# A recurrent attention block beside an MLP: both left query passes in the third segment of each four, and new orders of units and attention steps

## The chip, the cores and the metric

The kernel runs on one core of a Trainium2 chip. The metric is the time of one execution on the device in microseconds (us), read from the device. A core has a matrix engine (TensorE; PE in the profile, its weight loads PEld), two engines that work element by element (VectorE, here DVE, and ScalarE, here ACT), GpSimd (POOL), and SyncE (SP), which in this kernel only issues DMAs. PE writes its results to eight PSUM banks of 128 partitions x 512 float32 numbers. Sixteen DMA engines move data between the device's memory and the on-chip memory.

## The reference, cut to what matters

`x` has 2048 rows of 1024 numbers. Its layer norm `xn` goes into two branches, and the output is `x` plus both. Branch B is an MLP (1024 to 3584 to 1024, with a GELU). Branch A is a recurrence of 64 segments of 32 rows; each takes 8 memory rows from the one before. All tensors are bfloat16.

```python
for s in range(64):
    h = concatenate([mem, xn[32*s:32*s+32]])          # 8 + 32 rows of 1024
    q, k, v = h @ Wq, h @ Wk, h @ Wv                  # 32 heads of 128
    p = softmax(where(mask, q @ k.T / sqrt(128), -1e9))
    o = (p @ v) @ Wo                                  # back to 1024
    mem, out[s] = o[:8], o[8:]
return x + branch_A + gelu(xn @ w1 + b1) @ w2 + b2
```

Each of the four weight matrices of branch A has 1024 x 4096 numbers, 8 MB. Together they don't fit on the chip beside the rest, so a part of them is read again in every segment.

## The kernel before, in words

**Stages.** The first 402 us compute the layer norm and the MLP and store MLP plus `x` as rows to be added later. Then the 64 segments run one after the other, about 21.5 us each. The change lies in the segments (the loop over `s`, line 806 on).

**Units and passes.** The weights are cut into 64 units of 128 x 2048 numbers (512 KB). A segment uses them in seven passes: K half 0, Q half 0, K half 1, Q half 1, V half 0, V half 1, each of 8 units (`half_pass`, called as `K0`, `Q0`, `K1`, `Q1`, `V0`, `V1` in this text), and the output pass `O` with 16 units. A half is 16 of the 32 heads. One unit in a half pass is four matmuls of 32 rows, run beside each other in the four column groups of the PE array (`product`, line 830).

**Streamed and resident units.** 47 of the units stay on the chip for good. 17 are streamed in each segment: 15 by DMA, issued by SP into a ring of six slots, and two that are kept in four PSUM banks and copied by DVE into a slot (`copy_bits`, line 273, two copies of 128x512 for a unit). A slot is filled again as soon as PE has used its unit (`unit_done`, `start_stream`). The table `PLACED` says for each kind of segment at which places of each pass the streamed units stand (eight strings of eight places: the six half passes and the two halves of `O`; "S" is a streamed unit). Within a pass, units may stand in any order, since they are summed.

**Main rows and left rows.** A segment's 40 rows are not all multiplied in the segment itself. The 8 memory rows and the first 24 rows of `xn` make the 32 columns of `hT` (tile `hr_home`): the main rows. The last 8 rows of `xn` of four segments, which don't depend on the recurrence, are put together into one tile of 32 columns, `hL` (tile `hrL`): the left rows of a group. Each group of four segments therefore has, besides the four main passes of each kind, one left pass for K0, Q0, K1, Q1, V0 and V1, made for the group ahead (queries, keys) or at its beginning. A left pass has no weight traffic of its own: each unit is used a second time by four more matmuls while it is in its slot.

**The four kinds of segment.** `i4` is the segment's number modulo 4, and I call it the kind. The left passes are spread over the kinds:

| kind | left passes before | also |
|---|---|---|
| 0 | K1, V0 | |
| 1 | Q0 | the left outputs: `O` for 64 rows, not 32 |
| 2 | Q1 | |
| 3 | K0, V1 | |

Left queries of a group are held in `qL[0]` and `qL[1]`, four slots of 8 rows each. When the left pass of the next group overwrites them, slots not used yet must be saved: `keep_q` copies them into spare columns of the PSUM tile `mixed` (view `qS`), and `q_left` takes a segment's slot from `qL` or from `qS`.

**The boundary of two segments.** The last sum of `O` gives the 8 memory rows. They are added up (DVE, line 1224), turned into columns by two matmuls with an identity (`put_mem`, line 320), copied by DVE (line 330) into `hT`, and only then can the next segment's K0 begin. To fill that time, `lead_products` runs up to six resident units of a left pass of the next segment ahead: four before `put_mem` and two after it. Before the change this is done at all four boundaries of a group, with Q0, Q1, K0 and K1 left. In the last group there is nothing to lead with at the boundaries behind kinds 0, 1 and 2.

**The attention steps.** Between units PE does the small matmuls of the attention: `scores` (lines 947, 953), `sums` (985, 991) and `values` (1039, 1045), for each half. Between them ACT and DVE compute exponentials, minimum with a mask (line 977), normalised probabilities (lines 996, 999, 1012, 1017, 1024), the turned queries (`turn_q`: ACT copies at line 909, a transpose by DVE at line 914), and the copies of the values (line 1058). The left keys and queries are turned by `turn` (lines 882, 896). All engines work through their own instructions in the order in which the kernel is written down; there is no scheduler. After which unit a step stands is set by constants, one number for each kind: `SCORES_0` (in K1), `SUMS_0` (in Q1), `ATTEND` and `VALUES_0` (in V1; `attend` is `scores` of half 1 and the copy of V half 0), `SUMS_1` (in V1) and `VALUES_1` (in `O`).

**PSUM.** Three banks go round as accumulators (`new_acc`, `let_go`), one is `mixed`, four hold the kept units.

Of the kernel before, what the change touches and what calls it, by code (L numbers as in the profile page):

```python
# [11 lines left out]
U32 = mybir.dt.uint32  # L12
# [6 lines left out]
S = 2048  # L19
# [19 lines left out]
NL = SEG - NX  # L39
GRP = 4  # L40
# [14 lines left out]
MEM_AT = 20  # L55
EARLY_SEGS = 7
LEAD_FIRST = 4
SCORES_0 = (6, 6, 6, 5)
SUMS_0 = (4, 4, 4, 4)
ATTEND = (0, 0, 0, 1)  # L60
VALUES_0 = ((4, 4), (4, 4), (4, 4), (3, 5))
SUMS_1 = (6, 7, 6, 5)
VALUES_1 = (5, 5, 5, 5)
LATER = 4
# [9 lines left out]
def pass_order():  # L74
# [12 lines left out]

ORDER = pass_order()
PLACED = (
    "..SS...." ".S..S..." "S....S.." "....S..S" "....S..." "S..S...S" "...S..S." "S....S.S",  # L90
    "...SS..." ".S..S..." "..S..S.." "....SS.." ".S......" "S..S...S" "...S..S." "S....S.S",
    ".SS....." "S...S..." "S....S.." "....S..S" "....S..." "S..S...S" "...S..S." "S....S.S",
    "..SS...." ".S..S..." "S.....S." "....S..S" "....S..." "...SS..S" "...S..S." "S....S.S",
)
IS_STREAMED = {unit: PLACED[0][n] == "S" for n, unit in enumerate(ORDER)}
assert all(placed.count("S") == STREAMED for placed in PLACED)
# [24 lines left out]
def kernel(  # L121
# [52 lines left out]
    qL = [  # L174
        nc.alloc_sbuf_tensor_at(f"qL{u}", [P, 16, SEG], BF16, offset=SCRATCH + 1024 * (u + 1))[:, :, :] for u in range(2)
    ]
# [10 lines left out]
    def slab(place):  # L187
        if place in low:
            return low[place]
        return slabs.tile([P, 2048], BF16, name="u", tag=place)  # L190
# [8 lines left out]
    for j in range(4):  # L199
        q = slice(32 * j, 32 * j + 32)  # L200
# [148 lines left out]
    with tc.tile_pool(name="ma", bufs=2) as ma:  # L349
# [39 lines left out]
        for i in range(14):  # L389
            t = slab(f"w2_{i}")[:, :].rearrange("p (c d) -> p c d", d=DM)  # L390
# [14 lines left out]
        def next_of(ring):  # L405
            ring.rotate(-1)
            return ring[-1]
# [177 lines left out]
        for tg in range(4):  # L585
            last = tg == 3
            if last:
# [3 lines left out]
                h = 4 * IN_BANKS[1] + 2 * IN_BANKS[2]  # L591
# [12 lines left out]
            for fb in range(FC):  # L604
# [9 lines left out]
                u = next_of(us)  # L614
# [67 lines left out]
            else:  # L682
# [32 lines left out]
                for step in range(FC + AHEAD):  # L715
                    for t in range(4):
# [3 lines left out]
                        for nb in range(2):  # L720
                            n = 2 * t + nb
# [14 lines left out]
    with tc.tile_pool(name="late", bufs=1) as late:  # L736
# [18 lines left out]
        mixed = banks.tile([P, 512], F32, name="mixed", tag=f"bank{seg_banks[3]}")  # L755
# [4 lines left out]
        qS = there[:, 0:32 * NL].rearrange("p (i h t) -> p i h t", i=2, h=16)  # L760
# [42 lines left out]
        for s in range(NSEG):  # L803
            g, i4 = divmod(s, GRP)
            first, final = s == 0, s + 1 == NSEG
# [7 lines left out]
            more = g + 1 < NGRP  # L813
            units = ORDERS[i4]
            O_UNITS = units[48:]
            left_k = [first or (i4 == 3 and more), i4 == 0]
            left_q = [first or (i4 == 1 and more), first or (i4 == 2 and more)]
            left_v = [i4 == 0, first or (i4 == 3 and more)]
            left_o = i4 == 1 or final
            og, slot = divmod(s + 2, GRP)  # L820
# [97 lines left out]

            def q_left(u):

                if i4 >= 2 + u and more:
                    q = qS[:, i4 - 2 - u, :, :]
                else:
                    q = qL[u][:, :, NL * i4:NL * i4 + NL]
                nc.vector.tensor_copy(out=q_home[:, :, 0:NL], in_=q)
# [4 lines left out]

            def keep_q(u):

                n = 2 - u
                copy_bits(
                    mixed[:, 340:340 + 64 * n].bitcast(U32).rearrange("p (i h t) -> p h i t", i=n, h=16),
                    qL[u].bitcast(U32)[:, :, (GRP - n) * NL // 2:].rearrange("p h (i t) -> p h i t", i=n),
                )

            def scores(u):
# [191 lines left out]
            if left_q[0] and not first:  # L1131
                turn_qL(psQL, 0)
            psK1, psK1L = half_pass("K", 1, left_k[1], {SCORES_0[i4]: [lambda: scores(0)]})
            exps(0)
# [4 lines left out]
            }  # L1139
            at[4 if first else SUMS_0[i4]] = [lambda: sums(0)] + ([] if first else [lambda: q_left(1)])  # L1140
            if left_q[1] and not first:
# [25 lines left out]

            at = {0 if first else ATTEND[i4]: [attend]}
            n0, n1 = (3, 5) if first else VALUES_0[i4]
            if n0 == n1:  # L1170
# [29 lines left out]
            for n, unit in enumerate(O_UNITS):  # L1200
                t = unit_tile(unit)
# [13 lines left out]
            if not final:  # L1215
                o_sb = outM
                no = 16 if left_o else 8
                o = psX[:, 0:32 * no].rearrange("p (h e) -> p h e", e=32)
                if left_o:
                    nc.scalar.copy(out=o_sb[:, 0:no, :], in_=o)  # L1220
                else:
                    o = psX[:, 0:256].rearrange("p (h e) -> p h e", e=16)
                    flat = o_sb.rearrange("p h e -> p (h e)")[:, 0:256].rearrange("p (h e) -> p h e", e=16)
                    nc.vector.tensor_tensor(out=flat, in0=o, in1=st["folded"], op=ALU.add)
                ahead = []
                if (i4 == 3 or more) and not final:
                    hL = nxt["hL"]
                    w, u = (("Q", 0), ("Q", 1), ("K", 0), ("K", 1))[i4]
                    ahead = [i for i in range(KT) if not IS_STREAMED[w, i, u]][:LEAD]
                    after = [i for w_, i, u_ in ORDERS[(s + 1) % GRP][:48] if (w_, u_) == (w, u)]  # L1230
                    order = ahead + [i for i in after if i not in ahead]
                    led.update(next=(w, u, new_acc(), ahead, order), made=0)
                    lead_products(LEAD_FIRST)
                put_mem(o_sb, nxt["hT"], mixed[:, 224:288], 4 // nw)
                if led:
                    lead_products(LEAD)
# [21 lines left out]
            if final:  # L1258
                engines = [nc.sync, nc.scalar]
                n = 0  # L1260
# [56 lines left out]
```

## Time and profile before

Three executions took 1789.95, 1795.13 and 1798.88 us, a median of 1795.13 us. The profiled execution took 1796.11 us, its span from the first to the last instruction 1794.4 us.

| what | of the profiled execution |
|---|---|
| PE busy | 1696.3 us, 95% of the span |
| PE weight loads | 889.3 us, 50% |
| DVE busy | 983.8 us, 55% |
| ACT busy | 683.6 us, 38% |
| POOL busy | 300.4 us, 17% |
| DMA | 594.44 MB, mean 331 GB/s; 365 to 398 GB/s in the slices of the segments |
| first segment begins; second begins | 401.7 us; 434.7 us |
| length by kind 0, 1, 2, 3 (mean of segments 8 to 59) | 21.0, 23.3, 20.3, 21.6 us |
| PE idle by kind (the same segments) | 1.1, 1.5, 1.7, 1.1 us |
| granted PE clock | 1.00 |

A line of the trace's answers gives a start, a duration, engine, line, operation and tiles; "[0.53 <-DVE kq L914]" behind it is the engine's idle time before it and who ended it. Matmul ends are modelled, and matmuls of the four column groups overlap, so a row of 32 matmuls of a pass is read by its start to the next row's start.

### The profile page before, as it was taken

Reading aid. Unit: us, or ns where it says so; the run is one execution under the profiler, and the core shown is the slowest. Engines: PE = TensorE matmul, PEld = TensorE weight load, DVE = VectorE, ACT = ScalarE, POOL = GpSimd, SP = SyncE. Lnnn points to the kernel's source line nnn. Section 1 sums busy time; section 2 is a strip of 40 time slices with the busy share of each in tenths; the row PEclk is TensorE's granted clock in tenths of the full one; section 3 lists DMA queues with packets and bytes.
Section 4 is the critical chain, followed back from the end, with each engine's and each line's share of the span. In section 5 each row is a group of like instructions: output and inputs, shape, how many; then the busy total and the mean of one; then the engine's idle time right before and its main releaser. Section 6 shows DMA issues by size and latency. Waiting matters only on the chain.

```text
span 1794.4 us, 71508 instructions
## 1 busy us (share of the span) xinstructions
PE 1696.3 (95%) x31164; PEld 889.3 (50%) x31164; DVE 983.8 (55%) x2514; ACT 683.6 (38%) x1692; POOL 300.4 (17%) x586
## 2 busy tenths in 40 slices
PE   9999999999999999999999999999999989999988
PEld 5444444444555555545454555554545544554544
DVE  7656483825555555555455555555555554555544
ACT  6344251603333333334343434343434333433333
POOL 0000002301231111212122121121121111111111
PEclk9999999999999999999999999999999999999999
DMA  9455312789999999999999999999999999999998
GB/s 279 144 169 165 87 48 73 267 277 371 391 385 383 387 376 384 377 379 382 365 394 371 390 386 398 378 393 372 374 382 384 385 371 369 380 383 381 370 386 316
DMA packets 232830, 594.44 MB, mean 331 GB/s; under 512 B 57715, under 2 KB 88035, under 8 KB 232516
## 3 DMA queue, kind: packets, MB, share of 16 engines
q1 hardware_dynamic: 197584, 567.08, 84.4%
q0 software_dynamic: 16896, 16.85, 2.9%
q10 hardware_dynamic: 18036, 5.94, 1.3%
q8 instruction: 244, 4.00, 0.9%
q14 instruction: 70, 0.57, 0.1%
HBM read 573.43 MB, written 28.90 MB: 336 GB/s over the span
## 4 chain that ended last, share of the span: by engine, by line
PE 75%; DMA 11%; ACT 4%; DVE 4%; issue 4%; ACTq 1%; SPq 1%; POOL 0%; DVEq 0%; POOLq 0%
PE acc L830 38%; PE acc L1088 12%; PE ps L534 10%; DMA u<-Wc_O 8%; PE ps L662 6%; PE ps L693 3%; DMA u<-Wc_V 2%; ACT mixed L999 2%; PE acc L1039 1%; PE mixed L947 1%; DVE kq L914 1%; ACTq L459 1%; DVE pd_main L1012 1%; ACT kq L909 1%; SPq L521 1%
## 5 line engine op out<-in xcount | busy, mean ns | idle before, releaser
L830 PE MATMUL acc<-u,hr_home 128*32 128x512 bf16 x11520 | 758.8, 380 | 14.7 <-issue 8.3
L830 PEld LDWEIGHTS <-hr_home 128*32 128x32 bf16 x12288 | 350.3, 96 | 281.1 <-issue 33.2
L830 PE MATMUL acc<-u,hrL 128*32 128x512 bf16 x2880 | 256.2, 380 | 2.6 <-DVE qL L882 1.0
L534 PE MATMUL ps<-u 128*128 128x512 bf16 (+1 forms) x992 | 195.0, 358 | 0.0
L273 DVE TENSOR_SCALAR u<-kept 128x512 uint32<-128x512 uint32 x254 | 163.2, 684 | 56.9 <-PE acc L830 43.2
L1088 PE MATMUL acc<-u,d_oL 128*32 128x512 bf16 x2592 | 168.9, 380 | 13.1 <-issue 7.9
L882 ACT CAST d_oL<-acc 128x512 bf16<-128x512 f32 x143 | 82.0, 584 | 256.8 <-PE acc L830 251.5
L1088 PE MATMUL acc<-u,kq 128*32 128x256 bf16 (+1 forms) x2884 | 135.8, 310 | 13.6 <-DMA u<-Wc_O 11.2
L662 PE MATMUL ps<-u 128*128 128x512 bf16 x672 | 146.0, 379 | 0.0
L534 PEld LDWEIGHTS <-u 128*128 128x128 bf16 x992 | 91.6, 98 | 101.5
L1088 PEld LDWEIGHTS <-kq 128*32 128x32 bf16 x3908 | 103.0, 96 | 75.4 <-ACT kq L1058 21.2
L1012 DVE TENSOR_TENSOR pd_main<-kq,mixed 128x320 bf16<-128x320 bf16 x128 | 62.5, 488 | 130.2 <-ACT mixed L999 130.2
L914 DVE STREAM_TRANSPOSE kq<-kq 128x512 bf16<-128x512 bf16 x128 | 91.0, 711 | 73.2 <-ACT kq L909 71.0
L909 ACT CAST kq<-acc 128x512 bf16<-128x512 f32 (+2 forms) x192 | 85.4, 445 | 112.2 <-PE acc L830 82.6
L1279 POOL DMA_DIRECT2D out_dram<-hr_home x168 | 85.4, 516 | 221.7 <-DVE hr_home L1246 221.7
L886 ACT CAST kq<-acc 128x512 bf16<-128x512 f32 x128 | 75.2, 588 | 112.2 <-PE mixed L953 112.2
L830 PEld LDWEIGHTS <-hrL 128*32 128x32 bf16 x3072 | 87.9, 96 | 58.5 <-issue 7.6
L977 DVE TENSOR_TENSOR kq<-kq,mixed 128x96 bf16<-128x96 bf16 (+1 forms) x256 | 38.1, 190 | 125.8 <-ACT kq L967 72.6
L662 PEld LDWEIGHTS <-u 128*128 128x128 bf16 x672 | 65.5, 98 | 78.8 <-DVE u L619 0.4
L611 ACT ACTIVATE u<-ps,b1col 128x512 bf16<-128x512 f32 x112 | 76.5, 684 | 65.4 <-PE ps L534 62.3
L1088 PEld LDWEIGHTS <-d_oL 128*32 128x32 bf16 x2592 | 64.6, 96 | 67.7 <-issue 20.8
L999 ACT ACTIVATE mixed<-mixed,small_consts 128x160 f32<-128x160 f32 x256 | 94.2, 368 | 8.4
(126 smaller groups left out, 1911.2 us busy)
## 6 DMA issues: line engine op xcount, KB each, us to landing
u<-Wc_K SPq DMA_DIRECT2D x256, 512.0 KB
u<-Wc_V SPq DMA_DIRECT2D x256, 512.0 KB
u<-Wc_O SPq DMA_DIRECT2D x256, 512.0 KB
u<-Wc_Q SPq DMA_DIRECT2D x192, 512.0 KB
u<-in_B_w_dram SPq DMA_DIRECT2D x28, 512.0 KB
u<-in_A_Wq_dram SPq DMA_DIRECT2D x13, 512.0 KB
u<-in_A_Wv_dram SPq DMA_DIRECT2D x12, 512.0 KB
u<-in_A_Wk_dram SPq DMA_DIRECT2D x9, 512.0 KB
```

The costliest lines, as they stand in the source:

```text
L273: nc.vector.tensor_single_scalar(out=out, in_=in_, scalar=0, op=ALU.bitwise_or)
L534: nc.tensor.matmul(ps[:, SEG * s0:SEG * s1].rearrange("p (s t) -> p s t", t=SEG), lhsT=w1_sb[fb // 2][:, kt, (fb % 2) * P:(fb % 2 + 1) * P ...
L611: nc.scalar.activation(out=xb[:, :], in_=ps[:, :], func=ACT.Identity, bias=b1col[:, fb:fb + 1], scale=1.0)
L662: nc.tensor.matmul(ps[:, :], lhsT=gts[fc // 4][:, fc % 4, t * P:(t + 1) * P], rhs=w2_sb[fc // 2][:, fc % 2, cs], start=(fc == 0), stop=(fc ...
L830: nc.tensor.matmul(o, lhsT=lhs[:, i, :], rhs=m, start=(i == seq[0]), stop=(i == seq[-1]), tile_position=(0, 32 * j),)
L882: cp(out=out, in_=ps.rearrange("p (h e) -> p h e", e=32))
L909: nc.scalar.copy(out=q_home[:, h0:h1, NL:40], in_=ps[:, 32 * h0:32 * h1].rearrange("p (h e) -> p h e", e=32))
L914: nc.vector.transpose(out=home, in_=home)
L999: nc.scalar.activation(out=mixed[:, 160 * b:160 * b + 160], in_=mixed[:, 0:160], func=ACT.Exp, scale=-1.0, bias=off[:, b:b + 1],)
L1012: nc.vector.tensor_tensor(out=pdA.rearrange("p c b q -> p b c q"), in0=prA[:, None, :, :].to_broadcast([P, 2, 4, 40]), in1=dd, op=ALU.mult,)
L1088: nc.tensor.matmul(acc[r0:r0 + rows, 0:256 * len(blocks)], lhsT=lhsT, skip_group_check=True, rhs=o_columns(t, k, blocks), start=start, sto ...
L1279: loads.dma_start(out=out_flat[rows, 256 * j:256 * j + 256], in_=res[32 * j:32 * j + NX, :])
```

## The change

Both left query passes of a group now run in kind 2; kind 1 keeps only the left outputs. With that, `keep_q` saves one slot of each half (before: two of half 0 and one of half 1), and only kind 3 reads saved slots. The boundary behind kind 0 has no lead any more; the boundary behind kind 1 leads with Q0 (before: Q1). So six unit products go out of one boundary of each group and into kind 2's Q1 pass.

Beside that the places of streamed units move within passes (Q1 and both halves of `O` above all, K0 in kind 3, Q0 in kind 1), and attention steps by one unit: `scores` of half 0 in kind 3 one later, `sums` of half 0 in kinds 1 and 2 one earlier, `attend` in kind 1 one later, `values` of half 0 in kind 0 one earlier. The same number of units is streamed, by the same DMAs; which of the units of Q1 and `O` are streamed differs.

```diff
-SCORES_0 = (6, 6, 6, 5)
-SUMS_0 = (4, 4, 4, 4)
-ATTEND = (0, 0, 0, 1)
-VALUES_0 = ((4, 4), (4, 4), (4, 4), (3, 5))
+SCORES_0 = (6, 6, 6, 6)
+SUMS_0 = (4, 3, 3, 4)
+ATTEND = (0, 1, 0, 1)
+VALUES_0 = ((3, 3), (4, 4), (4, 4), (3, 5))
 PLACED = (
-    "..SS...." ".S..S..." "S....S.." "....S..S" "....S..." "S..S...S" "...S..S." "S....S.S",
-    "...SS..." ".S..S..." "..S..S.." "....SS.." ".S......" "S..S...S" "...S..S." "S....S.S",
-    ".SS....." "S...S..." "S....S.." "....S..S" "....S..." "S..S...S" "...S..S." "S....S.S",
-    "..SS...." ".S..S..." "S.....S." "....S..S" "....S..." "...SS..S" "...S..S." "S....S.S",
+    "..SS...." ".S..S..." "S....S.." "S......S" "....S..." "S..S...S" "....SS.." "S..S...S",
+    "...SS..." ".S.....S" "..S..S.." "S...S..." ".S......" "S..S...S" ".....SS." ".S...S.S",
+    ".SS....." "S...S..." "S....S.." "S.....S." "....S..." "S..S...S" ".....SS." "S.....SS",
+    "S..S...." ".S..S..." "S.....S." "S......S" "....S..." "...SS..S" ".....SS." "S....S.S",
 )
-            left_q = [first or (i4 == 1 and more), first or (i4 == 2 and more)]
+            left_q = [first or (i4 == 2 and more)] * 2
             def q_left(u):
-                if i4 >= 2 + u and more:
-                    q = qS[:, i4 - 2 - u, :, :]
+                if i4 == 3 and more:
+                    q = qS[:, u, :, :]
             def keep_q(u):
-                n = 2 - u
                 copy_bits(
-                    mixed[:, 340:340 + 64 * n].bitcast(U32).rearrange("p (i h t) -> p h i t", i=n, h=16),
-                    qL[u].bitcast(U32)[:, :, (GRP - n) * NL // 2:].rearrange("p h (i t) -> p h i t", i=n),
+                    mixed[:, 340 + 64 * u:404 + 64 * u].bitcast(U32).rearrange("p (h t) -> p h t", h=16),
+                    qL[u].bitcast(U32)[:, :, (GRP - 1) * NL // 2:],
                 )
-                if (i4 == 3 or more) and not final:
+                if i4 and (i4 == 3 or more) and not final:
                     hL = nxt["hL"]
-                    w, u = (("Q", 0), ("Q", 1), ("K", 0), ("K", 1))[i4]
+                    w, u = (None, ("Q", 0), ("K", 0), ("K", 1))[i4]
```

## The prediction

> **What bounds the kernel now.** I read first the page's busy shares and the chain of work that ended last.
>
> ```profile
> PE 1696.3 (95%) x31164; PEld 889.3 (50%) x31164; DVE 983.8 (55%) x2514; ACT 683.6 (38%) x1692; POOL 300.4 (17%) x586
> ...
> PE 75%; DMA 11%; ACT 4%; DVE 4%; issue 4%; ACTq 1%; SPq 1%; POOL 0%; DVEq 0%; POOLq 0%
> ```
>
> PE is busy 95% and holds three quarters of the chain; DMA is the only other large holder. Then four consecutive segments, kinds 0 to 3 (columns: stretch, length, busy time of PE, PEld, DVE, ACT, POOL, granted clock, DMA share, GB/s).
>
> ```profile
> 1185.70:1206.70 21.00, 19.77 (x466) 11.08 (x466) 11.71 (x31) 8.35 (x23) 3.70 (x7) 1.00 1.01 389
> 1206.70:1229.80 23.10, 21.73 (x472) 11.08 (x472) 10.62 (x29) 7.71 (x21) 3.71 (x7) 1.00 0.99 374
> 1229.80:1250.60 20.80, 18.71 (x434) 10.22 (x434) 12.47 (x33) 7.86 (x22) 4.70 (x9) 1.00 1.02 380
> 1250.60:1272.40 21.80, 20.32 (x466) 11.30 (x466) 11.16 (x30) 9.04 (x24) 3.79 (x7) 1.00 1.00 373
> ```
>
> DMA shares near 1 say that DMA could be the bound as well. Which of the two sets the length shows in the spread of the groups: cut at the first product of each kind 0, the 13 groups of segments 8 to 59 take 83.7 to 89.8 us. Waits of PE that the profile puts down to nothing ("issue") fill 0.35 us of the shortest and 5.9 us of the longest, and over all 13 a group grows by 1.04 us for each microsecond of them. Both groups fetch the same bytes. If DMA set the pace it would swallow such stalls; so PE's own path does, and its waits add up. These are the waits, of 13.2 groups:
>
> ```profile
> PE acc L1088 <- DMA u<-Wc_O: 11.7, 22, 1.3
> PE mixed L947 <- DVE kq L914: 10.9, 34, 0.5
> PE acc L830 <- issue: 10.5, 14, 1.8
> ...
> PE acc L1039 <- ACT kq L882: 5.3, 12, 0.5
> PE acc L1039 <- DVE pd_main L1012: 4.3, 16, 0.5
> ...
> PE acc L830 <- DMA u<-Wc_V: 2.0, 4, 0.9
> ```
>
> DMA waits are 13.7 us, 1.03 a group, nearly all in V1 and `O` of kind 2, the kind with the least PE work. The L914 waits (`scores` waiting for turned queries) are 0.82 a group: 0.40 in kind 1, 0.23 in kind 2, 0.20 in kind 3. Last, the boundary behind kind 0, with a lead, and in the last group without, and then the boundary behind kind 2 there:
>
> ```profile
> 1204.30 1.04 PE L1088 MATMUL acc<-u,kq 128*32 128x256 bf16 x32
> 1205.17 1.04 PE L830 MATMUL acc<-u,hrL 128*32 128x512 bf16 x16
> ...
> 1206.73 0.82 PE L830 MATMUL acc<-low,hr_home 128*32 128x512 bf16 x12
> ...
> 1724.46 1.05 PE L1088 MATMUL acc<-u,kq 128*32 128x256 bf16 x32
> 1726.25 0.21 PE L320 MATMUL mixed<-ident_mem,kq 128*128 128x32 bf16 x2 [0.73 <-DVE kq L1224]
> 1726.78 0.83 PE L830 MATMUL acc<-low,hr_home 128*32 128x512 bf16 x12 [0.32 <-DVE hr_home L330]
> ...
> 1766.80 0.84 PE L1088 MATMUL acc<-u,kq 128*32 128x256 bf16 x24
> ...
> 1768.71 0.61 PE L830 MATMUL acc<-low,hr_home 128*32 128x512 bf16 x8 [0.32 <-DVE hr_home L330]
> ```
>
> From the end of `O` to K0's first product: 1205.34 to 1206.73 is 1.39 us with six units of lead inside, 1725.51 to 1726.78 is 1.27 us with none. Lead costs the boundary 0.12 us; six units elsewhere cost six times 0.216 (a pass of eight takes 1.73 us from start to start).
>
> **The change part by part**, for one group, on PE's path. Fifteen groups have it.
>
> *Boundary behind kind 0:* 1.39 becomes 1.27, -0.12. There is a little more. In kind 0 DVE is late for the add of line 1224 (it starts 0.26 us after `O`, since two adds of line 1109 end at 1205.50); behind kind 2 it starts 0.06 us after, and the boundary takes 1768.71 - 1767.64 = 1.07 us. In the new order of kind 0 streamed units stand at places 4 and 5 of `O`, so the two PSUM copies (1.28 us) come before DVE's copies of the values, not between those and the adds, and the adds come earlier. I take -0.31, bounds -0.12 and -0.31. The price: the right half's values are ready about 1.87 us after the probabilities, and `O`'s thirteenth unit, the first to need them, comes after 1.88 us. I take nothing, at most 0.3.
>
> *Kind 1, Q0:* two left products go, -0.43.
>
> *Kind 2:* Q0 gains two left products (the other six are led at the boundary, as Q1's were), +0.43; Q1 has eight instead of two, +1.30. Together +1.73. So the work itself costs 1.73 - 0.43 - 0.31 = +0.99 us a group, because six products that ran for 0.12 us now run at full price.
>
> *L914 waits.* Kind 1: `sums` stands one unit earlier and `attend` one later, so the chain from `sums` to `scores` has 0.43 us more cover against waits of 0.47 us (11 of 13 segments). That `sums` can stand earlier needs DVE's `qL` copy and transpose (0.65 and 0.71 us) out of kind 1, which the change does. Kind 2: Q1's four units behind `sums` take 0.43 us each, which covers the mean 0.30 us. Kind 3: `scores` one unit later covers its 0.20 us. I take -0.35, -0.23 and -0.20, -0.78 in all; bounds -0.83 and -0.40, if DVE's moved 1.36 us makes half of it come back in kind 2.
>
> *DMA waits of kind 2.* PE comes to V1 and `O` 1.73 us later, and places 3 and 6 become 5 and 6. The waits there were at most 1.3 us, so they go: -1.03. But DMA must deliver: from 4 KB packets of SP's queue, 128 to a unit, I read how long a unit lies ready before its use. Where PE waits it is 1.2 to 1.4 us; in V0 and V1 of kind 1 the median is 1.6 to 1.9 us, and PE will arrive there about half a microsecond earlier. I let 0.15 come back: -0.88, bounds -1.03 and -0.30.
>
> *Waits that appear.* In kind 2 some DMA waits hid the chain to `values` in `O`; it waits 0.17 us now and 0.33 us in kind 0, where nothing hides it: +0.2. In kind 0 `values` after three units meets a value copy that needs 0.7 us against 0.65 us of cover, and `attend` in kind 1 does the same: +0.15 for both. Bounds 0 and 0.5.
>
> *Nothing for:* `keep_q` (0.28 and 0.23 us of DVE; one slot less; DVE is at 55%), `q_left` (0.15 to 0.23 us), PSUM banks (Q1's second bank is freed by DVE 2.17 us into K1 and needed after 2.29 us). SP issues the same fifteen DMAs, only at moved uses; POOL's and ACT's queues keep their order. If DVE came 0.1 us later in K1, the bank would be the next wait.
>
> *Sum:* +0.99 - 0.78 - 0.88 + 0.35 = -0.32 us a group, times 15 is -4.8. The sum goes against the profiled execution: 1796.1 - 4.8 = 1791.3. That execution lies 1.0 us above the median, less than the spread of the three runs. Low end: 0.99 - 0.83 - 1.03 + 0 = -0.87, -13 us: 1783. High end: 0.99 + 0.19 + 0.3 - 0.40 - 0.30 + 0.5 = +1.28, +19 us: 1815.
>
> **The rivals.**
>
> *Waits move to kind 1 (slower).* The place is V0 and V1 of kind 1, where units lie ready only 1.6 us before use. If the 0.5 us that PE gains before it takes the reserve under 1.2 us, DMA waits of kind 2 come back there: a third of the gain from them is left (-0.30) and half of that from L914 (-0.40): 0.99 - 0.70 + 0.35 = +0.64 a group, about 1806. It decides when more than 0.4 us of the reserve goes. For it: DMA shares of 0.99 to 1.02. Against: kind 1's `O` takes 9.6 us for four streamed units, and kind 2 now gives DMA 0.7 us more.
>
> *Everything is paid back (faster).* All DMA and L914 waits go and no wait appears: -0.87 a group, and a trifle more if smaller gaps go with them: 1782.
>
> *DMA sets the pace.* The bytes are the same, so the time is: 1796. For it the DMA shares, against it the 1.04.
>
> *The clock.* A boundary without lead idles PE in two pieces of 0.73 and 0.32 us. If that halved the granted clock for the next two passes (3.46 us), each boundary would cost 3.46 us more, 52 us in all: 1843. Against it: the last group runs three such boundaries at a granted clock of 1.00. The Trainium skill has such a rule (TensorE: Matmul & The Clock Gate, section "A second HAM failure mode: psum-queue depth-cycling"): short PE idles between groups of matmuls make the clock go down and up again. This trace doesn't agree at gaps of this size.
>
> **How the numbers follow.** Main case 0.46, alone 1785 to 1798; fully paid back 0.23; waits moved 0.21; DMA's pace 0.08; clock 0.02. The predicted time is the main case's, 1791. A change of 0.5% (9 us) is about what a measurement here can tell from none. Below 1786: nearly all of the paid-back case and a quarter of the main case, 0.35. Above 1804: most of the moved waits and the clock, 0.20. The rest, 0.45. Eight in ten reach from 1779 (the low end and half the spread of the runs) to 1807 (the moved waits); beyond lie the tails of both and the clock.
>
> **What would show it.** Right: at the boundary behind kind 0, K0's first product 1.07 to 1.27 us after `O` with PE idle about 1 us; kind 1 shorter by about 1 us with the boundary counted, kind 2 longer by 0.5 to 1; waits on Wc_O under 3 us in all in segments 8 to 59 (now 11.7), L914 under 2 (10.9); L1039 on L1012 nearer 7 (4.3). Wrong: DMA waits in V0 or V1 of kind 1, waits of L830 on DVE L882 in Q1 of kind 2 (the bank), or a wait in `O` of kind 0 for line 1057.

## The result, and the profile after

The changed kernel takes 1805.64 us (median of ten executions, 1795.7 to 1816.76) against 1795.64 us (ten executions, 1784.61 to 1799.22) of the kernel before: a ratio of 1.0067 with an interval of [1.0044, 1.0089], slower by 10 to 12 us. The prediction was 1791 us, 4.8 us faster.

The profiled execution took 1800.16 us with a span of 1798.4 us. It lies 5.5 us under the median, so the two profiles differ by only 4 us. The page of the changed kernel, busy shares and chain:

```profile
PE 1704.6 (95%) x31164; PEld 894.2 (50%) x31164; DVE 981.2 (55%) x2514; ACT 683.4 (38%) x1692; POOL 299.1 (17%) x586
...
PE 53%; DMA 12%; issue 3%; ACT 2%; DVE 2%; DVEq 0%; ACTq 0%; SPq 0%
```

PE issues the same 31164 matmuls and is busy for 8.3 us more (1696.3 before). The chain's shares add up to 72% here and to all of the span before, so the walk back ended earlier, and the fall from 75% to 53% isn't a reading of the change.

The same four segments 36 to 39 as in the prediction, now of the changed kernel (columns as there):

```profile
1191.70:1212.38 20.68, 19.06 (x442) 10.50 (x439) 11.53 (x30) 8.34 (x23) 3.68 (x7) 1.00 1.02 392
1212.38:1234.49 22.11, 21.58 (x460) 11.58 (x464) 9.49 (x26) 7.70 (x21) 3.69 (x7) 1.00 1.01 391
1234.49:1255.33 20.84, 19.92 (x467) 11.43 (x467) 13.66 (x36) 7.93 (x22) 4.69 (x9) 1.00 1.01 378
1255.33:1277.45 22.12, 20.59 (x468) 10.81 (x467) 11.18 (x30) 8.93 (x24) 3.78 (x7) 1.00 1.00 370
```

This group is 0.95 us shorter than before (85.75 against 86.70). A single group says nothing here: groups of one execution spread over several microseconds. The sum has to be made over many. First the 52 segments 8 to 59 as one stretch, of the kernel before and then of the changed kernel:

```profile
585.71:1705.99 1120.28, 1050.62 (x23691) 571.41 (x23691) 599.00 (x1548) 428.54 (x1170) 206.83 (x390) 1.00 1.00 380
```

```profile
586.29:1710.91 1124.62, 1058.02 (x23690) 575.60 (x23690) 596.40 (x1547) 428.51 (x1170) 206.05 (x390) 1.00 1.00 379
```

PE's idle time fell by 3.1 us (69.66 to 66.60), its busy time rose by 7.4. To get past the luck of one execution I pool three profiles of each kernel, the two above and those of the kernels with 32 and 64 small matmuls put ahead (described below, else unchanged): 39 groups on each side. A group then takes 85.91 us before and 86.74 us after, +0.83; fifteen groups make 12.4 us, which is the measured loss. By kind, as the prediction's terms add up for each kind, and as measured:

| kind | predicted | before, us | after, us | measured |
|---|---|---|---|---|
| 0 | -0.24 | 21.18 | 21.03 | -0.15 |
| 1 | -0.56 | 22.98 | 22.71 | -0.26 |
| 2 | +0.67 | 20.30 | 21.07 | +0.78 |
| 3 | -0.20 | 21.46 | 21.93 | +0.47 |

Kind 2, where the work was added, came out nearly as worked out. More than half of the miss lies in kind 3, which has no more work than before, and a quarter in kind 1. The waits of PE in 13.2 groups of the changed kernel, the answer of the same stretch as in the prediction:

```profile
PE acc L830 <- issue: 10.0, 19, 1.1
PE acc L1087 <- DMA u<-Wc_O: 7.4, 18, 1.3
PE acc L1087 <- issue: 7.3, 15, 1.2
PE mixed L320 <- DVE kq L1223: 7.1, 13, 0.7
PE mixed L952 <- issue: 6.8, 9, 1.8
PE acc L1038 <- ACT kq L882: 4.7, 10, 0.5
PE acc L1038 <- DVE pd_main L1011: 4.3, 17, 0.3
PE acc L830 <- DVE hr_home L330: 4.1, 13, 0.3
...
PE acc L830 <- DMA u<-Wc_Q: 2.1, 7, 0.7
...
PE mixed L946 <- DVE kq L914: 0.2, 1, 0.2
```

(Lines behind 933 have moved up by one: L946 was L947, L1038 was L1039, L1087 was L1088, L1223 was L1224.) The L914 waits are gone, 10.9 us to 0.2. Waits on Wc_O went from 11.7 to 7.4 us, and they stand in another kind now: in kind 0's `O`, mostly before its units at places 5 and 11, counted from 0 (0.57 us five times, 0.36 us nine times), and no longer in kind 2. Waits on Wc_Q are new: eight times 0.27 us before the fifth unit of Q1 in kind 1 (the list leaves out stretches under 0.15 us). L320 and L330 are the open boundary.

**What idle time hides.** These lists count idle stretches of PE, and an idle stretch is shorter than the wait that made it. A row of four matmuls of a half pass is drawn 0.38 to 0.41 us long, but the next row starts 0.216 us after it (0.108 us for the rows of 256 columns in `O`). A row that starts up to about 0.17 us late therefore leaves no idle time: the wait shows as busy time. V1 of kind 1 in segment 37 of the changed kernel, from the last row of V0 on, three rows to a line, with attention steps between the lines:

```profile
1221.69 0.83 PE L830 MATMUL acc<-u,hr_home 128*32 128x512 bf16 x12
...
1222.57 0.99 PE L830 MATMUL acc<-u,hr_home 128*32 128x512 bf16 x12
...
1224.54 0.92 PE L830 MATMUL acc<-u,hr_home 128*32 128x512 bf16 x12
```

Three rows take 0.83 us where none is late. In the second line one row is 0.16 us late, in the third one is 0.08 us late. Both late rows belong to streamed units (places 3 and 7) and start as a transfer of Wc_V lands, and neither has idle time before it. So the waits have to be counted again, from row start to row start: each step from a row to the next, less 0.216 or 0.108 us, put down to what released the late row, and idle stretches everywhere else. The waits for transfers are then 1.73, 1.93 and 1.92 us a group in the three profiles before and 1.82, 1.49 and 2.04 us in the three after. As a mean they fall by 0.07 us, where idle time shows a fall of 0.23. Kind 2 lost 1.17 us of them; kind 0 got 0.51 (0.41 of it in `O`), kind 1 0.49 (0.25 in Q1, 0.20 at V units) and kind 3 0.10. In kind 1, 38 rows were late for a V unit in the three profiles before, and 81 after.

### The profile page after: what moved, and what is told of

Same layout as the page of the kernel before. It is cut to its first block, busy times and chain, and to the rows that moved or that the text cites. A ratio compares the mean times of both kernels' runs of the same rounds, so it can differ in the third digit from the quotient of the medians.

```text
span 1798.4 us, 71498 instructions
## 1 busy us (share of the span) xinstructions
PE 1704.6 (95%) x31164; PEld 894.2 (50%) x31164; DVE 981.2 (55%) x2514; ACT 683.4 (38%) x1692; POOL 299.1 (17%) x586
## 4 chain that ended last, share of the span: by engine, by line
PE 53%; DMA 12%; issue 3%; ACT 2%; DVE 2%; DVEq 0%; ACTq 0%; SPq 0%
PE acc L830 37%; PE acc L1087 12%; DMA u<-Wc_O 7%; DMA u<-Wc_Q 3%; DMA u<-Wc_V 2%; PE acc L1038 1%; ACT mixed L998 1%; PE mixed L946 1%; DVE pd_main L1011 1%; PE mixed L320 1%; PE mixed L952 1%; PE acc L1044 1%; ACT mixed L995 0%; DVE kq L1016 0%; ACT kq L882 0%
## 5 line engine op out<-in xcount | busy, mean ns | idle before, releaser
L830 PE MATMUL acc<-u,hr_home 128*32 128x512 bf16 x11520 | 782.2, 380 | 14.4 <-issue 6.6
L830 PEld LDWEIGHTS <-hr_home 128*32 128x32 bf16 x12288 | 343.3, 96 | 293.6 <-issue 33.8
L830 PE MATMUL acc<-u,hrL 128*32 128x512 bf16 x2880 | 268.5, 380 | 4.0 <-issue 2.2
L1087 PE MATMUL acc<-u,d_oL 128*32 128x512 bf16 x2592 | 169.4, 380 | 9.4 <-issue 4.9
L1087 PE MATMUL acc<-u,kq 128*32 128x256 bf16 (+1 forms) x2884 | 136.7, 312 | 8.3 <-DMA u<-Wc_O 5.3
L1087 PEld LDWEIGHTS <-kq 128*32 128x32 bf16 x3908 | 105.1, 97 | 70.3 <-ACT kq L1057 22.8
L914 DVE STREAM_TRANSPOSE kq<-kq 128x512 bf16<-128x512 bf16 x128 | 91.0, 711 | 74.0 <-ACT kq L909 72.1
L830 PEld LDWEIGHTS <-hrL 128*32 128x32 bf16 x3072 | 92.5, 97 | 61.9 <-issue 10.7
L1087 PEld LDWEIGHTS <-d_oL 128*32 128x32 bf16 x2592 | 65.7, 96 | 67.2 <-issue 18.5
```

Of the source, the lines that this page charges most:

```text
L830: nc.tensor.matmul(o, lhsT=lhs[:, i, :], rhs=m, start=(i == seq[0]), stop=(i == seq[-1]), tile_position=(0, 32 * j),)
L914: nc.vector.transpose(out=home, in_=home)
L1087: nc.tensor.matmul(acc[r0:r0 + rows, 0:256 * len(blocks)], lhsT=lhsT, skip_group_check=True, rhs=o_columns(t, k, blocks), start=start, sto ...
```

## The boundary behind kind 0

The boundary from segment 36 to 37 of the changed kernel, PE and then DVE in order of time:

```profile
1210.48 0.84 PE L1087 MATMUL acc<-u,kq 128*32 128x256 bf16 x24
1211.85 0.21 PE L320 MATMUL mixed<-ident_mem,kq 128*128 128x32 bf16 x2 [0.53 <-DVE kq L1223]
1212.38 0.83 PE L830 MATMUL acc<-low,hr_home 128*32 128x512 bf16 x12 [0.32 <-DVE hr_home L330]
```

```profile
1210.25 0.85 DVE L1108 TENSOR_TENSOR d_oL<-acc,d_oL 64x256 f32<-64x256 f32 x2 [0.56 <-ACT d_oL L1105]
1211.37 0.42 DVE L1223 TENSOR_TENSOR kq<-acc,d_oL 128x256 bf16<-128x256 f32 x1 [0.27 <-PE acc L1087]
```

`O` ends at 1211.32, and K0 begins 1.06 us later: 1.39 before. DVE is free 0.22 us before `O` ends, and its add starts 0.05 us after. This step of the prediction (1.07 us, -0.31) holds to 0.02 us.

## The experiments

Several theories had to be told apart. The loss could lie in the moved pass or in the new orders; in the open boundary or a clock that falls with it; in transfers that come late in other places (the theory A of the expectations: waits move); in where the instruction stream's blocks happen to fall; or in a rule that a wait taken from PE's path isn't time won, because another one was hidden in it.

**The pass alone.** The changed kernel, with the places (all four rows) and the steps of before.

```diff
-SCORES_0 = (6, 6, 6, 6)
-SUMS_0 = (4, 3, 3, 4)
-ATTEND = (0, 1, 0, 1)
-VALUES_0 = ((3, 3), (4, 4), (4, 4), (3, 5))
+SCORES_0 = (6, 6, 6, 5)
+SUMS_0 = (4, 4, 4, 4)
+ATTEND = (0, 0, 0, 1)
+VALUES_0 = ((4, 4), (4, 4), (4, 4), (3, 5))
 PLACED = (
-    "..SS...." ".S..S..." "S....S.." "S......S" "....S..." "S..S...S" "....SS.." "S..S...S",
+    "..SS...." ".S..S..." "S....S.." "....S..S" "....S..." "S..S...S" "...S..S." "S....S.S",
...
```

> The moved left pass alone: left queries, saved slots and the lead as in the changed kernel, but places of units and attention steps as before. Theory A (the DMA waits of kind 2 only change places, because DMA delivers no faster; the six products that lost their boundary are the price): 0.99 us a group of new PE work (0.33 of the boundary's gain needs the new places of kind 0, so rather 1.2), kind 2 wins its L914 wait of 0.23, kind 1 keeps most of its L914 wait, and DMA waits come to about 1 us a group as before: slower than the kernel before by 0.5 to 1.0%, 1804 to 1814 us against 1796. Theory B (the new places of units make the waits, the pass is harmless): 1793 to 1799, not slower than before.

Measured 1806.89 us, ratio 1.0073 [1.0045, 1.0100]: the pass alone costs as much as the whole change. Its waits, in the same stretch:

```profile
PE mixed L320 <- DVE kq L1223: 8.7, 13, 0.7
...
PE acc L830 <- DMA u<-Wc_V: 4.0, 13, 1.1
PE mixed L946 <- DVE kq L914: 3.9, 16, 0.5
...
PE acc L1087 <- DMA u<-Wc_O: 2.8, 6, 0.7
PE acc L830 <- DMA u<-Wc_Q: 2.4, 5, 0.7
```

With no new order at all, Wc_O fell from 11.7 to 2.8 us and L914 from 10.9 to 3.9. So most of the idle stretches that the prediction counted as won go through the pass itself. The loss is 13 us all the same, 0.87 us a group, nearly the +0.99 us of added work. Waits on Wc_V and Wc_Q stand where there were few: from row start to row start the waits for transfers are 1.61 us a group, 1.06 us of them in kind 1 (0.23 to 0.59 before). They have moved there. (This profile is of the slowest execution, 9 us above the median.)

**The orders alone.** The kernel before, with the new steps and all four rows of the new places: the edit of the last kernel the other way round.

```diff
-SCORES_0 = (6, 6, 6, 5)
-SUMS_0 = (4, 4, 4, 4)
-ATTEND = (0, 0, 0, 1)
-VALUES_0 = ((4, 4), (4, 4), (4, 4), (3, 5))
+SCORES_0 = (6, 6, 6, 6)
+SUMS_0 = (4, 3, 3, 4)
+ATTEND = (0, 1, 0, 1)
+VALUES_0 = ((3, 3), (4, 4), (4, 4), (3, 5))
 PLACED = (
...
```

> The new places of units and attention steps alone, with the left query passes and the leads as before. Theory A: the L914 waits of kind 3 (0.20 us a group) and a part of those of kind 1 go, a value copy in kind 0 costs 0.14, the rest is a shift of DMA waits: between -0.4% and +0.1% of the kernel before, 1789 to 1798 us. Theory B: the new places cost what the changed kernel lost: slower by 0.4 to 0.8%, 1803 to 1810, with waits for units in Q1 of kind 1 and O of kind 0.

Measured 1802.55 us, ratio 1.0043 [1.0019, 1.0068]. Without the pass the orders do harm, although the L914 waits fall to 0.2 us here too. Waits for transfers are 2.57 us a group here, from row start to row start, 0.7 us more than before, which takes back what L914 gave. About 4 us of the 8 can be the clock's, as an estimate that lets the time go with it: this kernel's executions had a mean granted clock of 0.9964, those of before 0.9987. The two parts, +0.73% and +0.43%, don't add up to the whole, +0.67%: the orders give a little back only when the pass is there.

**Work thrown away in the boundary.** The changed kernel, with six products of Q0 left put back into the boundary behind kind 0, for nothing (Q0 left still runs whole in kind 2).

```diff
+thrown = i4 == 0 and more
+if thrown:
+    hF = nxt["hL"]
+    fill = [i for i in range(KT) if not IS_STREAMED["Q", i, 0]][:LEAD]
+    psF = new_acc()
+    for i in fill[:LEAD_FIRST]:
+        product("Q", i, res_tiles["Q", i, 0], hF, psF, fill)
 put_mem(o_sb, nxt["hT"], mixed[:, 224:288], 4 // nw)
+if thrown:
+    for i in fill[LEAD_FIRST:]:
+        product("Q", i, res_tiles["Q", i, 0], hF, psF, fill)
+    let_go(psF)
```

> The changed kernel, with six products of left queries run at the boundary behind kind 0 and thrown away, so that PE doesn't idle there. Theory C (a part of the loss is the granted clock, which falls to half for 3.4 us here and there because the open boundary leaves PE idle): granted clock back at 1.000 in nearly all runs, and although the boundary takes 0.33 us more in 15 groups (5 us) the time is that of the changed kernel or less, 1800 to 1806 us. Without C: clock as in the changed kernel (0.996 to 0.999) and 5 us more than it, about 1810.

Measured 1810.11 us, ratio 1.0106 [1.0086, 1.0125], 4.5 us above the changed kernel's median (7 us by the ratios). The idle boundary isn't what hurts: filling it makes the kernel slower, by 0.3 to 0.5 us a group, with the prediction's 0.12 to 0.31 at the lower side of that. Its granted clock, 0.9987 as a mean over its runs, is that of before. Nor does the clock explain the change: the mean is 0.9987 before and 0.9979 after, which is 1.4 us.

**Three units fewer a segment, before and after.** From segment 1 on, K unit (2,0), V unit (3,1) and O unit (4,0) take the weights of a resident unit, so that SP issues 12 transfers a segment and not 15. All other work stays.

```diff
+NOT_FETCHED = {("K", 2, 0): ("K", 0, 0), ("V", 3, 1): ("V", 1, 1), ("O", 4, 0): ("O", 0, 0)}
 def unit_tile(unit):
     nonlocal used
+    if s and unit in NOT_FETCHED:
+        return res_tiles[NOT_FETCHED[unit]]
     if IS_STREAMED[unit]:
```

> The kernel before with 12 units by DMA in a segment instead of 15: from segment 1 on, one unit each of K0, V1 and O is not fetched, and a resident unit of the same pass is multiplied in its place, so the result is another. PE's work stays the same. Theory A (DMA is near its limit, so a DMA wait that is removed comes back elsewhere): the waits for units (14 us in segments 8 to 59) go, and little else: 1776 to 1784 us, 0.5 to 1.0% faster than before.

> The changed kernel with the same three units not fetched (the same part of the computation is left out). Theory A: now its DMA waits can't come back, and what is left of its loss is PE's own path: 0.99 us a group of work and 0.14 for the values of kind 0, less L914 waits of about 0.8, plus 0.2 for the probabilities in kind 2, so about +0.3 to +0.5 us a group: 4 to 8 us slower than the kernel before with fewer units (instead of 10 to 12 with all units). Rival D (the loss is not DMA's at all, but work and waits on PE, DVE and ACT): 10 to 12 us slower as with all units.

Measured 1761.97 us (ratio 0.9822 [0.9795, 0.9849]) and 1779.63 us (0.9911 [0.9887, 0.9935]). Waits of PE in the kernel of before, and then in the changed one (their lines are shifted by up to six):

```profile
PE mixed L953 <- DVE kq L920: 12.8, 39, 0.5
...
PE acc L836 <- DMA u<-Wc_V: 0.2, 1, 0.2
```

```profile
PE mixed L324 <- DVE kq L1229: 9.1, 13, 0.7
...
PE acc L836 <- DVE hr_home L334: 4.1, 13, 0.3
PE acc L836 <- DMA u<-Wc_V: 3.0, 7, 1.2
...
PE mixed L952 <- DVE kq L920: 0.2, 1, 0.2
```

I had expected the distance to shrink to 4 to 8 us with late transfers out of the way. It didn't: it is 17.7 us by the medians and 16 by the ratios, where it was 10 to 12. With six executions of each kernel, and about 5 us to either side, it is clear that the distance didn't shrink, not that it grew. That decides two things. Late transfers alone are not the cause, since they are nearly gone and the loss is still there. And the waits for transfers in kind 2 had been a real discount: without them the added pass there costs +1.22 us (19.73 to 20.95) where it had cost 0.78. What remains is puzzling at first: 12.6 us of L914 waits went (they are the rows L953 and L952 on L920 here), 0.95 us a group, which by the prediction's arithmetic would have paid for nearly all of the added work of 0.99 us; yet a group of these two profiles is 0.79 us longer. (That is 12 us over fifteen groups, less than the medians say: this profile of the kernel before is of its slowest execution, with four half-clock stretches in these segments against one.) From row start to row start, waits without a named cause ("issue", below: unnamed) rose from 2.08 to 2.59 us a group, waits for transfers from 0.06 to 0.33. These two together are 0.78 us. Kind 1 gained 0.45 us, little more than its two products. Kind 3 lost only 0.09 us here and 0.47 with all transfers: that its loss needs the full stream of weights is suggested by this one pair, not shown.

**A part of the orders.** The kernel before, with the new places of `O` in kinds 2 and 3 and `scores` one unit later in kind 3.

```diff
-SCORES_0 = (6, 6, 6, 5)
+SCORES_0 = (6, 6, 6, 6)
...
-    ".SS....." "S...S..." "S....S.." "....S..S" "....S..." "S..S...S" "...S..S." "S....S.S",
-    "..SS...." ".S..S..." "S.....S." "....S..S" "....S..." "...SS..S" "...S..S." "S....S.S",
+    ".SS....." "S...S..." "S....S.." "....S..S" "....S..." "S..S...S" ".....SS." "S.....SS",
+    "..SS...." ".S..S..." "S.....S." "....S..S" "....S..." "...SS..S" ".....SS." "S....S.S",
```

> The kernel before with only those new orders that shortened a segment in the traces: the places of kinds 2 and 3 in O, and scores of half 0 in kind 3 one unit later. Theory A: kind 3 wins its L914 wait of 0.20 us a group; in kind 2 the waits for units in O (1.0) are put off by two units, but DMA delivers no faster, so they come back in part in kinds 3, 0 or 1: 1785 to 1793 us, same or up to 0.5% faster than before. If places alone could remove DMA waits: 1783 or less.

Measured 1792.73 us, ratio 0.9996 [0.9974, 1.0018]: no difference. L914 fell from 10.9 to 6.1 us and Wc_O from 11.7 to 8.9; the waits on Wc_V rose from 2.0 to 5.7 us. From row start to row start the waits for transfers are 1.85 us a group, as before, and the unnamed ones are too (2.98 and 2.99 us).

**Kind 0 as before.** The changed kernel, with the places of kind 0's `O` and its `values` step as before, since the new waits on Wc_O stood there.

```diff
-VALUES_0 = ((3, 3), (4, 4), (4, 4), (3, 5))
+VALUES_0 = ((4, 4), (4, 4), (4, 4), (3, 5))
...
-    "..SS...." ".S..S..." "S....S.." "S......S" "....S..." "S..S...S" "....SS.." "S..S...S",
+    "..SS...." ".S..S..." "S....S.." "S......S" "....S..." "S..S...S" "...S..S." "S....S.S",
```

> The changed kernel with kind 0's places in O and its values step as before. Its trace showed a wait for a unit at the new place 11 of O in kind 0 (0.36 us a group) and a later value copy (0.14); the adds at the boundary become late again (+0.19). If these places are a cause of their own: 0.31 us a group less than the changed kernel, about 5 us: 1798 to 1802. Theory A in its pure form (a DMA wait removed in kind 0 shows up in kind 1): the time of the changed kernel within 2 us, 1803 to 1807, with longer waits for units in K1, Q1 and V0 of kind 1.

Measured 1807.13 us, ratio 1.0065 [1.0035, 1.0095]: nothing won. Its waits for transfers:

```profile
PE acc L830 <- DMA u<-Wc_V: 3.4, 5, 1.2
PE acc L830 <- DMA u<-Wc_Q: 3.2, 6, 1.5
...
PE acc L1087 <- DMA u<-Wc_O: 2.1, 6, 0.6
```

Of 7.4 us on Wc_O 5.3 went where they were attacked, 3.6 us came up at V and Q units instead, and the time is the same.

**Where the blocks of instructions fall.** Both kernels with 32 or 64 small matmuls at the very beginning, which moves every later instruction along the stream by a quarter or a half of the block described below.

```diff
 idle_products(WARM)
+for _ in range(32):
+    nc.tensor.matmul(idle[:, 0:8], lhsT=ident, rhs=ident[:, 0:8], start=True, stop=True)
```

> The kernel before with 32 tiny matmuls (64 PE instructions, under 2 us of PE, while it waits for the first rows) ahead of everything, so that every later PE instruction stands a quarter of a 16 KB block of instructions further on. In the traces nearly all unnamed stalls of PE lie on a grid of 127.5 matmuls, 255 PE instructions. Theory E (where that grid falls decides some us of each kernel's time by chance): it moves against the kernel before by more than 3 us, one way or the other. Theory F (the stalls cost the same wherever the grid falls, on average): 1792 to 1798 us, within 3 us of before.

> The changed kernel with the same 32 tiny matmuls ahead. Theory E: the distance to the kernel before with 32 matmuls is not 10 to 12 us but another, 3 to 6 us or 15 and more. Theory F: it stays slower than that kernel by 8 to 13 us, because the loss is made of steps that every group has, and of stalls that PE meets more often when it waits less.

> The same with 64 tiny matmuls (half a block). Theory E: over 3 us from the kernel before, either way. Theory F: 1792 to 1799 us.

> The changed kernel with 64 tiny matmuls ahead. Theory E: another distance to the kernel before with 64 matmuls than 10 to 12 us. Theory F: 8 to 13 us slower than it.

Measured, before: 1792.61 us (1.0001 [0.9980, 1.0022]) and 1796.37 us (1.0024 [1.0001, 1.0048]); after: 1805.24 us (1.0069 [1.0044, 1.0094]) and 1807.08 us (1.0088 [1.0058, 1.0117]). The distance is 12.6 and 10.7 us where it was 10: the loss isn't an accident of where blocks fall.

**Only the attention steps as before.** The changed kernel with its new pass and places, but the four constants of before.

```diff
-SCORES_0 = (6, 6, 6, 6)
-SUMS_0 = (4, 3, 3, 4)
-ATTEND = (0, 1, 0, 1)
-VALUES_0 = ((3, 3), (4, 4), (4, 4), (3, 5))
+SCORES_0 = (6, 6, 6, 5)
+SUMS_0 = (4, 4, 4, 4)
+ATTEND = (0, 0, 0, 1)
+VALUES_0 = ((4, 4), (4, 4), (4, 4), (3, 5))
```

> The changed kernel with the attention constants of before (SCORES_0, SUMS_0, ATTEND and VALUES_0), its new pass and its places of units kept. Theory P, a wait that is removed is time won: the score waits of kind 1 come back (+0.43 us a group), those of kind 3 (+0.21), and the values of kind 0 lose what their later start gave (-0.13), about +0.5 us a group, +7.5 us over the changed kernel, near 1813. Theory G, what the order takes from one wait comes back in waits for weight units and in stalls for instructions: no more than 3 us from the changed kernel to either side, 1803 to 1808. In the trace both expect the waits of the lines for the scores and values behind L914 to be back near those of before; G expects the unnamed stalls and the waits for DMA of segments 8 to 59 to be smaller by about as much as they grow.

Measured 1802.63 us, ratio 1.0054 [1.0033, 1.0074]. The changed kernel by its ratio is at 1.0067; the 7.5 us of theory P would have been 1.011. Its waits:

```profile
PE mixed L946 <- DVE kq L914: 6.6, 22, 0.5
PE acc L1038 <- DVE pd_main L1011: 5.4, 20, 0.5
...
PE acc L1087 <- DMA u<-Wc_O: 3.4, 9, 0.8
PE acc L830 <- DMA u<-Wc_Q: 2.5, 6, 0.9
PE acc L830 <- DMA u<-Wc_V: 2.1, 4, 1.1
```

6.4 us of L914 waits came back, and the kernel isn't slower for it; so theory P falls, and G's number holds. (The mean granted clock was 0.9995 here and 0.9979 in the changed kernel's executions. By the same estimate as above that is worth 2.9 us; without it the two kernels are level, 7.5 us short of what P expects.) G's account in the trace holds for the most part. Against the three pooled profiles of the changed kernel, from row start to row start, waits for engines are 0.66 us a group longer, waits for transfers 0.40 shorter and unnamed ones 0.11 shorter. This is one profile, and the unnamed waits spread by more than that from profile to profile.

## Why the prediction was wrong

Its sum was -0.32 us a group. The pooled profiles split the measured +0.83 in two ways: into PE's idle stretches of over 0.1 us and its busy time, and from row start to row start.

| part of a group, us | predicted | by idle time | by row starts | missed by (row starts) |
|---|---|---|---|---|
| waits for engines: open boundary +0.85, L914 -0.78, new ones +0.35 | +0.42 | +0.10 | +0.22 | -0.20 |
| waits for transfers | -0.88 | -0.23 | -0.07 | +0.81 |
| waits without a named cause | 0 | +0.37 | +0.42 | +0.42 |
| half-clock stretches (last section) | 0 | in the last row | +0.05 | +0.05 |
| the rest: moved products without the idle boundary, short idle stretches | +0.14 | +0.59 | +0.21 | +0.07 |
| sum | -0.32 | +0.83 | +0.83 | +1.15 |

*Work, +0.99: right.* The boundary took 0.33 us less, Q0 of kind 1 0.41 less, Q0 and Q1 of kind 2 0.43 and 1.30 more: +0.99.

*"I let 0.15 come back: -0.88": the step that failed, and most of the miss.* The waits for transfers did leave kind 2 (1.17 us a group by row starts). But 1.10 us came back elsewhere: 0.51 in kind 0, most of it in `O`, 0.49 in kind 1, 0.10 in kind 3. So 0.07 us were won and not 0.88, and this one term is 0.81 of the 1.15 us. The prediction looked for them in V0 and V1 of kind 1, where the ready time was 1.6 us. They are there (+0.20 us), mostly too short to leave idle time. The larger part is at places that it didn't price: kind 0's `O`, whose streamed units now stand beside each other at places 4 and 5, and Q1 of kind 1, whose units moved from places 4 and 5 to 0 and 4. I counted what PE's earlier arrival would do, not what the moved units would. The stream itself went no faster: 380 GB/s before and 379 after, at a DMA share of 1.00 in both.

*Unnamed waits, taken as unchanged: the step that failed second.* They rose by 0.83 us a group in kinds 2 and 3 and fell by 0.41 in kinds 0 and 1. For the two kinds this is firmer than one pair: by idle time, unnamed waits of kind 3 were 0.18 to 0.56 us in the five profiles with the old passes and 0.48 to 0.84 us in the seven with the new pass (all 15 units streamed); of kind 2, 0.23 to 0.44 against 0.45 to 0.68. As a sum over the kinds it is less firm: 1.31 to 2.50 against 2.31 to 2.77. V1 of kind 3, 5.11 us as a mean before, takes 5.44 after, and this alone is more than the 0.20 us that the later `scores` were to bring there.

*L914, -0.78: right in the trace, not as time won.* They went, 10.9 us to 0.2. But the last experiment let them come back and was no slower, with shorter waits for transfers. I had read the rule that a microsecond of wait is a microsecond of the group from the spread of the groups (1.04 us for each microsecond of unnamed waits), where it holds for stalls that come on top. It doesn't follow that a wait which is taken out is won: there, 0.66 us of waits for engines covered 0.40 us of waits for transfers.

*Waits that appear, +0.35: too much.* Apart from L914 and the boundary, waits for engines changed by -0.03 us in sum by idle time: they rose by 0.18 us in kind 2, where 0.2 was expected, and fell in kinds 0 and 3. Kind 0 shows no wait for line 1057, and the bank in Q1 of kind 2 was never late.

*PE busy.* By idle time PE is busy for 0.53 us a group more, and the moved products explain 0.14. Most of the difference is no work: it is the part of the waits that idle time hides, and 0.05 us are half-clock stretches (three in the three profiles after, one before, in segments 8 to 59). What is left, 0.07 us, has no place. The same holds for the kernel before, which is busy for 6.3 us less in these segments with 12 units than with 15: waits for transfers that show by row starts and not by idle time are 0.74 us a group with 15 units and 0.03 with 12. That is 9 us in thirteen groups, more than the 6.3, and the four half-clock stretches with 12 units work the other way.

*The rivals.* "Waits move to kind 1" (1806 us) has the right time and much of the right mechanism: the waits for transfers do come back, and its sign, waits in V0 and V1 of kind 1, did appear. But it let a third of that gain stand (-0.30, measured -0.07), it took half of the L914 waits to return, which they didn't do by name, and it knew nothing of `O` of kind 0, of Q1 of kind 1, or of the unnamed waits. That these errors cancel to within 1 us is luck. For its sake alone the eight in ten reached up to 1807, and the measured time lies just inside. "DMA sets the pace" falls as it was put: with the same bytes the time changed. The clock rule that the prediction weighed is not what happened; the half-clock stretches are a matter of one more in an execution, not one at each boundary.

*What stays open.* Why unnamed waits grow in kinds 2 and 3 and not in 0 and 1. What they are is told in the last section. That a wait for an engine gives a late block of instructions time to arrive, so that taking out the wait lays the block's lateness bare, would fit the pair with fewer units; in the last experiment the unnamed waits hardly changed. It is argued, not shown, and the rise in kinds 2 and 3 stays with the new pass whatever the steps.

No kernel here that computes the whole result beat the kernel before; the nearest, the part of the orders, equals it.

## What to carry to other kernels

Work that runs in a gap in which the engine must wait anyway is nearly free, and moving it to a place with waits of its own is not an even trade: price the moved work at its full duration, and price a wait that it covers at nothing until you have named what is late behind it. Where a stream of transfers runs at its limit (a DMA share near 1), waits for it move when units are reordered; count the sum over all stages, not the wait that you attack. Groups of one execution that spread by several microseconds can't carry a difference of one: pool profiles. And count waits from the start of one instruction to the start of the next: where instructions overlap, a wait shorter than the overlap shows as busy time.

## What the hardware showed that I had not expected

**Stalls at blocks of instructions.** PE's unnamed waits aren't scattered. Counted in matmuls, they lie on a grid of 127.5 (255 instructions with the weight loads), in both kernels. The page of the changed kernel has a queue for it (packets, MB, share of the engines' time):

```profile
q8 instruction: 244, 4.00, 0.9%
```

244 packets of 16 KB. Two such stalls of segment 51, in PE's order of time:

```profile
1521.52 0.17 PE L952 MATMUL mixed<-kq,d_oL 128*32 128x16 bf16 x1
1522.86 0.19 PE L952 MATMUL mixed<-kq,d_oL 128*32 128x16 bf16 x3 [1.16 <-issue]
...
1527.78 0.38 PE L830 MATMUL acc<-u,hr_home 128*32 128x512 bf16 x1
1529.07 0.40 PE L830 MATMUL acc<-u,hr_home 128*32 128x512 bf16 x3 [0.91 <-issue]
```

Each cuts a run of four like matmuls behind its first, and from one to the next are 128 matmuls. The packets of this queue started at 1520.50 and 1526.70, 2.36 and 2.37 us before PE went on. A block lasts PE about 6 us; its packet starts about 2.7 us after the crossing before it where there is no stall, and 3.8 us where there is one. With 12 units a segment the start comes earlier in the kernel before (2.1 to 2.8 us by kind, against 2.7 to 3.2 with 15), but not clearly in the changed one (2.5 to 3.2 against 2.9 to 3.1). All unnamed waits come to about 30 us in segments 8 to 59. The Trainium skill (Runtime: NRT & Kernel Launch, section "Instruction fetch mechanics") has the blocks of 16 KiB and 256 instructions, as the trace nearly does, and calls the cost of a crossing mostly hidden. Here it is not hidden: 59 waits of PE without a named cause in those 52 segments, up to 1.8 us each.

**Half-clock stretches.** The profiles show none to seven stretches with the granted clock at half before the end, of 3.41 us each: none in the kernel before, two with 64 matmuls ahead of it, one in the changed kernel, seven with the orders alone. That of the changed kernel, and the 3.4 us behind it:

```profile
1685.70:1689.10 3.40, 3.16 (x53) 2.30 (x56) 0.83 (x2) 0.00 (x0) 0.00 (x0) 0.51 0.93 370
1689.20:1692.60 3.40, 3.40 (x66) 1.51 (x62) 1.25 (x4) 0.00 (x0) 1.85 (x4) 1.00 0.93 335
```

The clock, third column from the right, reads 0.51 and then 1.00. The stretch begins while PE stands in an unnamed stall of 1.18 us (1684.76 to 1685.94). All 23 such stretches in the fourteen profiles begin within 1.6 us of the end of an idle stretch of PE of 0.9 to 2.7 us, while a stall of 1.86 us in the kernel before came without one. The Trainium skill (TensorE: Matmul & The Clock Gate, section "Why this matters for your kernels") asks for no idle gap of PE over about 3 us. Here a stall of 1.18 us came with a stretch at half clock, and thirteen open boundaries, with 0.85 us of idle time each, went by without one.
